# Loading part of the next sequence earlier in an attention and mixture-of-experts kernel, and moving two weight copies

## The chip, the cores and the metric

The kernel runs on one core of a Trainium2 chip. The metric is the device time of one execution in microseconds (us). The kernel before took 206.89 us (median of 3 executions, 206.02 to 209.92; with the fourth one that was taken beside the kernel after, 206.45). A core has five engines with their own instruction streams: TensorE for matrix multiplications, VectorE, ScalarE, GpSimd, and SyncE, which here only issues DMA. Data moves between HBM and on-chip memory (SBUF) over 16 DMA engines. These serve several queues. Two matter here. One is fed by SyncE (hardware queue, `q1`); it carries q, k, v and the outputs. The other is fed by GpSimd (software queue, `q0`); it carries the expert weights.

## The reference

Eight sequences of 576 tokens pass through attention with separate softmaxes on q and k, then through a mixture of experts (MoE) in which each whole sequence picks one of eight experts.

```python
q_s = softmax(q, over head_dim);  k_s = softmax(k, over the sequence)
kv  = einsum('bhsd,bhse->bhde', k_s, v)         # 64 x 64 per head
x   = einsum('bhsd,bhde->bhse', q_s, kv)        # -> (8, 576, 512)
pooled = x.mean(axis=1); e = argmax(pooled @ w_gate)   # one expert per sequence
out[b] = gate[b] * (relu(x[b] @ w1[e]) @ w2[e])  # w1 512x1024, w2 1024x512
```

## The kernel before

The kernel is one software pipeline. "Half n" means four heads of sequence n // 2, so halves 4 and 5 are sequence 2, and "load 4" brings q, k and v of half 4 (3 x 0.59 MB). While TensorE works on MoE of sequence b, the attention of sequence b + 1 is threaded between its matmuls. MoE b is cut into 17 pieces, and a table says which helper is emitted at which *tick*; ticks 17 b to 17 b + 17 belong to MoE b. Each engine's instructions stand in the program in the order in which the helpers emitted them, and an instruction that waits holds those behind it.

```python
    def load(n, names="qkv"):                    # SyncE: 3 DMAs into in_pool
        ...
    def cast_v(n, on_act=False):                 # GpSimd: v to 16 bit; waits for v's DMA
        ...
    def scale_q(n, eng):
        sum_q(n)                                 # VectorE: row sums, reciprocals (qsi)
        mul_q(n, eng)                            # GpSimd: eq * qsi, 2.12 us
    ...
    def load_w2(b):                              # GpSimd issues w2 of the expert of b, in two halves
        w2_src = moe_w2[ds(seqs[b]["e_val"], 1)].rearrange("o (c p) n -> p (o c) n", p=128)
        for hf in range(2):
            cs = slice(4 * hf, 4 * hf + 4)
            issued[b].append(
                nc.gpsimd.dma_start(out=w2_all[:, b % NS, cs], in_=w2_src[:, cs], **seqs[b]["kw"])
            )
        part_loads(b)
    ...
    def hold_loads(b):                           # SyncE reads a few bytes of w1 of b: SyncE waits until they are there
        nc.sync.dma_start(out=held, in_=w1_all[64:65, b, ND - 1, F - 8:F])
    ...
    def fetch(b, w_all, part):                   # VectorE: copies half of w1 or w2 from the slot where the expert lies
        ...
        copy = nc.vector.tensor_copy(
            out=w_all[:, b % NS, cs, fs],
            in_=w_all[:, ds(seqs[b]["src"], 1), cs, fs].rearrange("p o c f -> p (o c) f"),
        )
```

The weights stay in four slots. If the expert of sequence b lies in an older slot, no DMA is made and `fetch` copies it; if it was just loaded, the copy runs all the same, from the slot to itself. So TensorE always waits for the copy, and the copy waits for the DMA. The held read is the means of giving the weights the DMA engines first: SyncE, and all loads behind it, stand until w1 has landed.

The schedule that the change touches:

```python
    at_gate(0.2, 1)               # gate of sequence 1, and the issue of its w1 by GpSimd
    at(0.4, hold_loads, 1)
    at(0.4, load, 4)
    at(0.4, load, 5)
    at(0.4, load, 6)
    at(0.4, load, 7)
    ...
    at(13, load_w2, 1)
    ...
    places = [(20, 24.5), (29.7, 35), (41, 46), (56, 61), (73, 78), (90, 95)]
    for b in range(2, B):
        for i in range(2):
            n, t = 2 * b + i, places[b - 2][i]
            at(t, kvt_step, n)                    # TensorE: attention of half n
            ...
            at(t - 5.35, exp_q, n)
            at(t - (5.35 if n < 8 else 8), cast_v, n)
            at(t - 4.7, scale_q, n, nc.gpsimd)
        ...
        at_gate(places[b - 2][1] + (4.7 if b < 4 else 5), b)
    for b in range(1, B):
        for part in range(2):
            at(NU * b - 2.5 + 0.2 * part, fetch, b, w1_all, part)
            at((17.5, 38.3, NU * b + 4.5)[min(b, 3) - 1] + 0.2 * part, fetch, b, w2_all, part)
```

The softmax here doesn't subtract the row's maximum and nothing guards it: scores larger than these inputs give would overflow.

Of the kernel before, what the change touches and what calls it, by code (L numbers as in the profile page):

```python
# [19 lines left out]
def kernel(  # L20
# [15 lines left out]
    nc = tc.nc  # L36
# [3 lines left out]
    F = moe_w1.shape[2]  # L40
# [4 lines left out]
    ND = D // 128  # L45
# [17 lines left out]
    def bank(tag):  # L63
        return psum.tile([128, 1024 if tag == "x" else 512], FP32, name=tag, tag=tag, bufs=BUFS[tag])
# [17 lines left out]
    held = consts.tile([1, 8], FP16)  # L82
# [7 lines left out]
    w1_all = consts.tile([128, NS, ND, F], FP16, name="w1_all")  # L90
    w2_all = consts.tile([128, NS, NF, D], FP16, name="w2_all")
# [8 lines left out]
    def pair_src(t, b, i):  # L100

        return t[b].rearrange("(n i g) (p j) d -> i (g p) n (j d)", i=2, n=2, p=64)[i]
# [8 lines left out]
    def load(n, names="qkv"):  # L111
        if n >= 2 * B:
            return
        b, i = divmod(n, 2)
        for name in names:
            x = in_pool.tile([128, 2, J * Dh], FP32, name=f"{name}_in")
            nc.sync.dma_start(out=x, in_=pair_src({"q": q, "k": k, "v": v}[name], b, i))
            ins[n, name] = x.rearrange("p n (j d) -> p n j d", j=J)

    def exp_q(n):  # L120
        eq = e_pool.tile([128, J, 2, Dh], FP16, name="eq")
        nc.scalar.activation(out=eq.rearrange("p j n d -> p n j d"), in_=ins.pop((n, "q")), func=AF.Exp)  # L122
        halves[n] = {"eq": eq, "qt": {}, "kv": {}}

    def cast_v(n, on_act=False):
        dst = v_aug[n % NVB][:, :, 1:].rearrange("p j (n d) -> p n j d", n=2)
        if on_act:
            nc.scalar.copy(dst, ins.pop((n, "v")))
        else:
            nc.gpsimd.tensor_copy(out=dst, in_=ins.pop((n, "v")))  # L130

    def exp_k(n):
        ek = e_pool.tile([128, J, 2, Dh], FP16, name="ek")
        nc.scalar.activation(out=ek.rearrange("p j n d -> p n j d"), in_=ins.pop((n, "k")), func=AF.Exp)  # L134
        halves[n]["ek"] = ek

    def sum_q(n):
        qs = stat.tile([128, J, 2], FP32, name="qs")
        nc.vector.tensor_reduce(out=qs, in_=halves[n]["eq"], op=ALU.add, axis=AX.X)  # L139
        qsi = stat.tile([128, J, 2], FP32, name="qsi")  # L140
        nc.vector.reciprocal(out=qsi, in_=qs)  # L141
        halves[n]["qsi"] = qsi
        if n < 4:

            qhl = stat.tile([128, J, 2, 2], FP16, name="qhl")
            nc.vector.tensor_copy(out=qhl[:, :, 0], in_=qsi)
            nc.vector.tensor_tensor(out=qhl[:, :, 1], in0=qsi, in1=qhl[:, :, 0], op=ALU.subtract)
            halves[n]["qhl"] = qhl

    def mul_q(n, eng):  # L150
        eq, qsi = halves[n]["eq"], halves[n]["qsi"]
        eng.tensor_tensor(  # L152
            out=eq, in0=eq, in1=qsi.unsqueeze(3).to_broadcast([128, J, 2, Dh]), op=ALU.mult,
        )
# [57 lines left out]
    def kv_step(n):  # L212
        kv_mm(n)
        for g in range(2):
            kv_out(n, g)

    def t_step(n):
        t_mm(n)
        for g in range(2):
            t_out(n, g)  # L220
# [8 lines left out]
    def x_step(n, g):  # L229
        b, i = divmod(n, 2)  # L230
        c = 2 * i + g
        if c == 0:
            xt = xt_pool.tile([128, ND, S], FP16, name="xt")
            seqs.setdefault(b, {})["xt"] = xt
            if b > 1:
                seqs[b]["pooled"] = gat_pool.tile([128, ND], FP32, name="pooled")
        xt, pooled = seqs[b]["xt"], seqs[b].get("pooled")
        kvs, qts = halves[n]["kv"], halves[n]["qt"]
        px = bank("x")
        warm(FILL.get(("x", c, b), 0), px[:, 640:768])  # L240
        nc.tensor.matmul(px[:, 0:SM], lhsT=kvs[g], rhs=qts[g][:, 0:SM], start=True, stop=True)  # L241
        nc.tensor.matmul(px[:, SM:S], lhsT=kvs[g], rhs=qts[g][:, SM:S], start=True, stop=True)  # L242
        if b < 2:

            if c == 0 or n == 3:
                nc.vector.tensor_copy(out=xt[:, c, :], in_=px[:, 0:S])
            else:
                nc.scalar.copy(xt[:, c, :], px[:, 0:S])
        elif n < 8 and g:
            nc.scalar.activation(out=xt[:, c, :], in_=px[:, 0:S], func=AF.Copy, accum_out=pooled[:, c:c + 1])  # L250
        else:
            nc.vector.tensor_tensor_reduce(  # L252
                out=xt[:, c, :], in0=px[:, 0:S], in1=ones_f32.to_broadcast([128, S]),
                scale=1.0, scalar=0.0, op0=ALU.mult, op1=ALU.add, accum_out=pooled[:, c:c + 1],
            )

    def q_sum_step(n):


        b, i = divmod(n, 2)  # L260
        eq, qhl = halves[n]["eq"], halves[n]["qhl"]
        if i == 0:
            seqs.setdefault(b, {})["qb"] = [bank("mm"), bank("ht")]
            seqs[b]["qbar"] = gat_pool.tile([128, ND, 2, 4], FP16, name="qbar")
        qbar = seqs[b]["qbar"]
        warm(FILL["qsum", n], seqs[b]["qb"][1][:, 256:384])
        for g in range(2):
            c = 2 * i + g
            r = slice(64 * g, 64 * g + 64)
            qb = seqs[b]["qb"][g][:, 4 * i:4 * i + 4]  # L270
            for j in range(J):
                nc.tensor.matmul(
                    qb, lhsT=eq[r, j], rhs=qhl[r, j].rearrange("p h n -> p (h n)"), start=(j == 0), stop=(j == J - 1)
                )
            nc.vector.tensor_copy(out=qbar[:, c, 0], in_=qb)
            nc.vector.tensor_tensor(out=qbar[:, c, 1], in0=qb, in1=qbar[:, c, 0], op=ALU.subtract)
# [84 lines left out]
    def part_loads(b):  # L361
        for load_inst in issued[b]:
            for copy in copies.get(b - 1, ()):
                apart(load_inst, copy)

    def load_w2(b):
# [8 lines that stand above are left out]
    def warm(count, pw=None):  # L375

        if pw is None:
            pw = bank("ht")[:, 0:128]
        width = pw.shape[1]
        for n in range(count):  # L380
            nc.tensor.matmul(pw, lhsT=ident, rhs=blkmask[:, 0:width], start=True, stop=True)  # L381

    def hold_loads(b):

        nc.sync.dma_start(out=held, in_=w1_all[64:65, b, ND - 1, F - 8:F])

    def gate_exp(b):
        ex = gat_pool.tile([1, E], FP32, name="ex")
# [93 lines left out]
    NU = 17  # L482
    ticks = {}

    def at(t, fn, *args):
        ticks.setdefault(t, []).append((fn, args))
# [8 lines left out]
    at(2, t_step, 2)  # L495
    at_gate(0.2, 1)
    at(0.4, hold_loads, 1)
    at(0.4, load, 4)
    at(0.4, load, 5)
    at(0.4, load, 6)  # L500
    at(0.4, load, 7)
# [8 lines left out]
    at(0.3, gate_exp, 0)  # L510
    at(1.2, gate_value, 0)
    at(2.2, gate_spread, 0)
    places = [(20, 24.5), (29.7, 35), (41, 46), (56, 61), (73, 78), (90, 95)]
    for b in range(2, B):
        for i in range(2):
            n, t = 2 * b + i, places[b - 2][i]
# [11 lines left out]
    for b in range(1, B):  # L528
        for part in range(2):
            at(NU * b - 2.5 + 0.2 * part, fetch, b, w1_all, part)  # L530
            at((17.5, 38.3, NU * b + 4.5)[min(b, 3) - 1] + 0.2 * part, fetch, b, w2_all, part)
    times = sorted(ticks)
    done = [0]

# [13 lines left out]
    with tc.manual_schedule(engines={ET.PE, ET.DVE, ET.Activation, ET.Pool, ET.SP}):  # L548

        warm(80)  # L550
        exp_q(0)
        sum_q(0)
        q_sum_step(0)
        mul_q(0, nc.vector)
        exp_k(0)
        exp_q(1)
        cast_v(0)
        sum_q(1)
        load(3)
        t_step(0)  # L560
        q_sum_step(1)
        mul_q(1, nc.gpsimd)
        kv_step(0)
        exp_k(1)
        cast_v(1, True)
        x_step(0, 0)
        exp_q(2)
        kv_step(1)
        t_step(1)
        exp_k(2)  # L570
        pool_step(0)
        gate_step(0)
        x_step(0, 1)
        sum_q(2)
        exp_q(3)
        q_sum_step(2)
        x_step(1, 0)
        kv_mm(2)
        exp_k(3)
        x_step(1, 1)  # L580
        sum_q(3)
        for g in range(2):
            kv_out(2, g)
        cast_v(3)
        load_w2(0)
        q_sum_step(3)
        kv_step(3)
        for b in range(B):
            for m, _ in enumerate(moe(b)):
                run_ticks(NU * b + m + 1)  # L590
# [30 lines left out]
```

## Time and profile before

| | before |
|---|---|
| time, median | 206.89 us |
| span of the profiled execution | 204.1 us, granted clock 0.954 |
| TensorE busy | 178.6 us (88%) |
| MoE 0, 1, 2, 3 begin at | 27.45, 47.45, 77.36, 103.67 us |
| TensorE first uses w2 of sequence 1 at | 62.17 us |
| first half of w2 of sequence 1 landed, second half | 44.72, 47.31 us |

"MoE b begins" is the first w1 matmul of sequence b. Landings are the times at which the last of the 16 DMA engines raised the transfer's semaphore.

These rows of the profile's page cut the span into 40 slices of 5.1 us. A digit is the busy share in tenths, and PEclk is TensorE's granted clock in tenths:

```profile
PE   6798998995999839898869789999998899999990
PEclk9967899999699996999969999999999999999998
DMA  5999999999999799917999937966999967994055
```

TensorE is busy nearly everywhere, so a gain can only come from its few dips. The DMA engines are full without a break until about 66 us. The prediction shows the waits behind the dips.

### The profile page before, as it was taken

The page shows a single profiled execution, that of the slowest core. Times are in us where ns is not written, and L with a number is a line of the kernel's source. Part 1 is how long each engine was busy: PE and PEld are TensorE (multiplying, and loading weights), DVE is VectorE, ACT ScalarE, POOL GpSimd, SP SyncE. Part 2 cuts the span into 40 slices and gives each one's busy share as a digit, 9 for nine tenths or more (in the row PEclk, how much of TensorE's full clock was granted, in tenths as well). Part 3 has the DMA queues.
Part 4 walks back from the last instruction along what each step waited for, and adds up shares of the span by engine and source line. Part 5 has one row for each costly group of instructions (what it writes and reads, how often), then busy time and mean ns, then how long its engine had stood idle before and what let it go on. Part 6 is the DMA issues. An engine that isn't in the chain of part 4 may idle for free.

```text
span 204.1 us, 4940 instructions
## 1 busy us (share of the span) xinstructions
PE 178.6 (88%) x1882; PEld 101.8 (50%) x1882; DVE 115.6 (57%) x344; ACT 113.8 (56%) x182; POOL 64.3 (32%) x71
## 2 busy tenths in 40 slices
PE   6798998995999839898869789999998899999990
PEld 6776864443455424454335445555554455455440
DVE  0678877223667582997457666896689673121000
ACT  2668527744777644783437523982596146445540
POOL 2061915000763353347404260424175406000000
PEclk9967899999699996999969999999999999999998
DMA  5999999999999799917999937966999967994055
GB/s 180 378 389 391 165 167 194 184 213 392 394 386 358 163 347 405 390 39 110 230 295 296 365 98 189 328 189 226 267 315 202 206 137 126 197 207 168 0 112 122
DMA packets 29735, 48.58 MB, mean 238 GB/s; under 512 B 4112, under 2 KB 11280, under 8 KB 29712
## 3 DMA queue, kind: packets, MB, share of 16 engines
q1 hardware_dynamic: 19472, 37.76, 55.3%
q0 software_dynamic: 8544, 10.49, 31.7%
q10 hardware_dynamic: 1696, 0.02, 0.7%
q8 instruction: 15, 0.25, 0.5%
q14 instruction: 8, 0.07, 0.1%
HBM read 61.88 MB, written 9.44 MB: 349 GB/s over the span
## 4 chain that ended last, share of the span: by engine, by line
PE 41%; DMA 31%; DVE 16%; issue 4%; ACT 3%; POOL 0%; SPq 0%; ACTq 0%; POOLq 0%; DVEq 0%
PE mm L451 15%; PE mm L432 13%; DMA w_all<-in_moe_w_dram 13%; DMA q_in<-in_q_dram 9%; DMA v_in<-in_v_dram 5%; DVE qs L139 4%; DMA wg_sb<-in_moe_w_gate_dram 3%; DVE w_all L415 3%; PE mm L466 2%; DMA out_dram<-osb 2%; PE x L241 2%; PE kv L179 2%; DVE qt L209 2%; DVE kv L189 2%; PE ht L437 2%
## 5 line engine op out<-in xcount | busy, mean ns | idle before, releaser
L432 PE MATMUL mm<-xt,w_all 128*128 128x512 f16 x256 | 68.1, 397 | 4.8 <-DVE w_all L415 2.4
L451 PE MATMUL mm<-w_all,hsb 128*128 128x512 f16 x256 | 60.1, 379 | 0.0
L441 ACT ACTIVATE hsb<-mm 128x512 f16<-128x512 f32 x64 | 37.8, 595 | 21.7 <-PE mm L432 20.3
L458 ACT ACTIVATE osb<-mm,gate 128x512 f32<-128x512 f32 x32 | 22.0, 687 | 41.9 <-PE mm L451 37.3
L415 DVE COPY w_all<-w_all 128x2048 f16 x28 | 29.5, 1053 | 21.5 <-DMA w_all<-in_moe_w_dram 17.1
L451 PEld LDWEIGHTS <-hsb 128*128 128x128 f16 x256 | 22.9, 98 | 26.1
L152 POOL TENSOR_TENSOR eq<-eq,qsi 128x1152 f16<-128x1152 f16 x13 | 28.0, 2152 | 24.7 <-DVE qsi L141 22.1
L432 PEld LDWEIGHTS <-w_all 128*128 128x128 f16 x256 | 21.3, 101 | 24.6 <-issue 6.5
L130 POOL CAST va<-v_in 128x1152 f16<-128x1152 f32 x15 | 19.7, 1310 | 33.4 <-DMA v_in<-in_v_dram 33.3
L139 DVE TENSOR_REDUCE qs<-eq 128x18 f32<-128x1152 f16 x16 | 21.5, 1344 | 9.8 <-ACT eq L122 9.5
L437 PEld LDWEIGHTS <-w_all 128*128 128x128 f16 x256 | 16.8, 101 | 16.4 <-issue 2.2
L349 POOL DMA_DIRECT2D w_all<-in_moe_w_dram x18 | 8.3, 460 | 49.4 <-DMA w_all<-in_moe_w_dram 21.1
L122 ACT ACTIVATE eq<-q_in 128x1152 f16<-128x1152 f32 x16 | 18.5, 1159 | 6.9 <-DMA q_in<-in_q_dram 6.9
L241 PE MATMUL x<-qt,kv 128*128 128x512 f16 x32 | 12.6, 393 | 8.8 <-DVE pooled L252 6.5
L252 DVE CUSTOM_DVE_ANT_0 xt<-x,ones_f 128x576 f16<-128x576 f32 x20 | 14.8, 738 | 7.3 <-PE x L242 7.3
L134 ACT ACTIVATE ek<-k_in 128x1152 f16<-128x1152 f32 x16 | 18.6, 1162 | 0.5 <-DMA k_in<-in_k_dram 0.5
L437 PE MATMUL ht<-xt,w_all 128*128 128x64 f16 x256 | 18.4, 196 | 0.0
L381 PEld LDWEIGHTS <-ident 128*128 128x128 f16 x202 | 14.3, 116 | 2.5 <-POOL ident masks.py:199 1.6
L381 PE MATMUL ht<-blkmask,ident 128*128 128x128 f16 x170 | 13.5, 254 | 1.9 <-POOL blkmask L73 1.9
L179 PE MATMUL kv<-va,ek 64*128 64x129 f16 x288 | 11.9, 224 | 0.0
L189 DVE SCALAR_TENSOR_TENSOR kv<-kv,icv,blkmask 128x128 f16<-128x128 f32 x32 | 11.2, 351 | 1.2
L187 DVE RECIPROCAL icv<-kv 128x1 f32<-128x1 f32 x32 | 5.1, 159 | 10.9 <-PE kv L201 10.3
(77 smaller groups left out, 141.6 us busy)
## 6 DMA issues: line engine op xcount, KB each, us to landing
w_all<-in_moe_w_dram POOLq DMA_DIRECT2D x30, 512.0 KB
q_in<-in_q_dram SPq DMA_DIRECT2D x16, 576.0 KB, 6.1
k_in<-in_k_dram SPq DMA_DIRECT2D x16, 576.0 KB, 6.9
v_in<-in_v_dram SPq DMA_DIRECT2D x16, 576.0 KB, 8.4
out_dram<-osb SPq DMA_DIRECT2D x64, 128.0 KB, 5.6
w_all<-in_moe_w_dram POOLq DMA_DIRECT2D x4, 256.0 KB
out_dram<-osb_t SPq DMA_DIRECT2D x16, 64.0 KB, 2.8
gate<-gt ACTq DMA_DIRECT2D x8, 0.5 KB, 5.7
```

The source lines that it names most:

```text
L122: nc.scalar.activation(out=eq.rearrange("p j n d -> p n j d"), in_=ins.pop((n, "q")), func=AF.Exp)
L130: nc.gpsimd.tensor_copy(out=dst, in_=ins.pop((n, "v")))
L134: nc.scalar.activation(out=ek.rearrange("p j n d -> p n j d"), in_=ins.pop((n, "k")), func=AF.Exp)
L139: nc.vector.tensor_reduce(out=qs, in_=halves[n]["eq"], op=ALU.add, axis=AX.X)
L152: eng.tensor_tensor(out=eq, in0=eq, in1=qsi.unsqueeze(3).to_broadcast([128, J, 2, Dh]), op=ALU.mult,)
L381: nc.tensor.matmul(pw, lhsT=ident, rhs=blkmask[:, 0:width], start=True, stop=True)
L415: copy = nc.vector.tensor_copy(out=w_all[:, b % NS, cs, fs], in_=w_all[:, ds(seqs[b]["src"], 1), cs, fs].rearrange("p o c f -> p (o c) f"),)
L432: nc.tensor.matmul(phm, lhsT=w1_sb[:, c, fsl], rhs=xt[:, c, 0:SM], start=(c == 0), stop=(c == ND - 1),)
L437: nc.tensor.matmul(pht[:, fc * ST:(fc + 1) * ST], lhsT=w1_sb[:, c, fsl], rhs=xt[:, c, SM:S], start=(fc == 0 and c == 0), stop=(fc == NF - ...
L441: nc.scalar.activation(out=hsb[:, fc, 0:SM], in_=phm, func=AF.Relu)
L451: nc.tensor.matmul(po, lhsT=hsb[:, fc, st * 128:st * 128 + 128], rhs=w2_sb[:, fc, :], start=(fc == 0), stop=(fc == NF - 1),)
L458: nc.scalar.mul(osb, po, gate)
```

## The change

The intent was to remove the wait of 2.08 us near 50 us. Half 4 is to be loaded in the middle of the weights: a held read of the first half of w2 of sequence 0, then load 4, then the rest as before. Its attention moves from MoE 1 (ticks 20, 24.5) into the end of MoE 0 and early MoE 1 (17, 25). And the copies of w2 of sequences 1 and 2 move to ticks at which GpSimd is not scaling, since a VectorE copy and a GpSimd scaling stretch one another (in the kernel before, copies take up to 2.22 us beside a scaling and 0.69 alone, and a scaling 2.56 us beside copies and 2.12 alone).

```diff
     def hold_loads(b):
-        nc.sync.dma_start(out=held, in_=w1_all[64:65, b, ND - 1, F - 8:F])
+        src = w1_all[64:65, b, ND - 1, F - 8:F] if b else w2_all[64:65, 0, 0, 0:8]
+        nc.sync.dma_start(out=held, in_=src)
@@
     at(0.4, hold_loads, 1)
-    at(0.4, load, 4)
     at(0.4, load, 5)
@@
-    places = [(20, 24.5), (29.7, 35), (41, 46), (56, 61), (73, 78), (90, 95)]
+    places = [(17, 25), (30, 35), (42, 47), (57, 62), (73, 78), (90, 95)]
@@
-            at((17.5, 38.3, NU * b + 4.5)[min(b, 3) - 1] + 0.2 * part, fetch, b, w2_all, part)
+            at((23.7, 36.2, NU * b + 4.5)[min(b, 3) - 1] + 0.2 * part, fetch, b, w2_all, part)
@@
         load_w2(0)
+        hold_loads(0)
+        load(4)
```

Line `at(13, load_w2, 1)` is untouched. But the cast of v of half 4 is emitted 5.35 ticks before its attention and the scaling 4.7 ticks before. With the attention at tick 17 these fall on 11.65 and 12.3, ahead of 13. GpSimd's order changes without a line about it.

## The prediction

> **What bounds the kernel now.** I read the page first. Of a 204.1 us span TensorE is busy 178.6 us (88%), but the chain that ended last gives it only 41% and the DMA queues 31%. So TensorE is the floor, and what can be gained or lost are its idle stretches and what holds them. I then read the chain in order of time between 31 and 70 us (columns: start, length, what):
>
> ```profile
> 32.81 9.24 DMA w_all<-in_moe_w_dram
> 42.06 0.80 SPq L385
> ...
> 42.97 5.90 DMA q_in<-in_q_dram
> 48.89 1.16 ACT eq L122
> 50.05 0.39 ACT osb L458
> 50.45 12.47 DMA q_in<-in_q_dram
> 62.93 4.35 DMA out_dram<-osb
> 67.29 0.74 ACT xt L250 x2
> 68.08 0.36 PE x L296 x8
> ```
>
> From 22 to 66 us this is one stream of DMA: weights of sequences 0 and 1, the held read that waits for w1 of sequence 1 (42.06), four half-sequences of q, k, v, and the first outputs, whose buffers ScalarE needs again before it can evict x and gate 2 can run (68.08). The DMA windows show the stream without a hole: 192 GB/s in 36 to 44 us (the weight queue, counted after the cast to 16 bit, so about 385 of HBM reads), 393 GB/s in 47 to 63 us.
>
> Then TensorE in order of time, its long waits:
>
> ```profile
> 50.68 1.02 PE L432 MATMUL mm<-xt,w_all 128*128 128x512 f16 x4 [2.08 <-ACT osb L458]
> ...
> 76.91 0.58 PE L241 MATMUL x<-qt,kv 128*128 128x512 f16 x1 [3.65 <-DVE pooled L252]
> ...
> 103.67 1.89 PE L432 MATMUL mm<-xt,w_all 128*128 128x512 f16 x4 [2.44 <-DVE w_all L415]
> ```
>
> After each of the three the four matmuls take up to 1.9 us instead of 1.03 for some 3.4 us. The first is what the change goes for: ScalarE stands 3.37 us at exp of q of sequence 2, which landed at 48.89, and the eviction behind it holds TensorE. The second is the vector engine's copy of w1 of sequence 2, held by GpSimd's scaling:
>
> ```profile
> 73.52 2.12 POOL L152 TENSOR_TENSOR eq<-eq,qsi 128x1152 f16<-128x1152 f16 x1 [1.17 <-DVE qsi L141]
> ...
> 73.97 2.22 DVE L415 COPY w_all<-w_all 128x2048 f16 x1 [0.62 <-DVE qsi L141]
> ```
>
> The copy ends just after the scaling does; alone it takes 0.69 us. The third is w1 of sequence 3 landing at 102.8 us. After 120 us TensorE has about 1.3 us of gaps left, so what happens before 120 us is carried to the end.
>
> **What the Trainium skill says.** (1) "DMA: Bandwidth & Descriptors", section "Queues, rings and completion order": each DMA engine takes turns between the queues it has work for. The trace agrees; the DMA view of 102 to 112 us, in which weights and loads overlap:
>
> ```profile
> q1 hardware_dynamic: 967, 2.02, 58.7%
> q0 software_dynamic: 929, 0.93, 54.4%
> ```
>
> 0.93 MB of weights in 10 us (1.86 MB of HBM reads) beside 2.02 MB: equal shares, and a weight load takes twice its time alone. (2) "SBUF — State Buffer", section "SBUF: two separate sides": VectorE in a two-port mode and GpSimd exclude each other for a whole instruction. The 2.22 us copy above agrees. (3) "TensorE: Matmul & The Clock Gate", Part 1: after an idle window of some 3.4 us the clock is halved for a window. The trace has three such windows after 30 us, each of 3.4 us, behind the three waits above.
>
> **The change, part by part.** It adds one small held read; every other instruction stays, in another order. I read the order of the built program on each engine.
>
> (a) Load 4 (q, k, v of the first half of sequence 2, 3 x 0.59 = 1.77 MB) is issued when the first half of w2 of sequence 0 has landed, 33.1 us in the semaphore records, instead of 42.97. Data starts about 1.3 us after the issue at 34.0, so at 35.3. At that moment 0.88 MB of w1 of sequence 1 is left in the weight queue (1.75 MB of reads). Both share 0.387 MB/us, so both end near 44.6. The slowest engine lands 1.7 to 2.7 us after that (w1's 3.15 MB were through at 39.1 and landed at 42.05): w1 of sequence 1 and v at about 46.8, q at 41, k at 44. Exp of q then runs at 43.8 without a wait, and the 2.08 us hole with its slow window, some 4 us, goes.
>
> (b) The price is in GpSimd's order. Before, w2 of sequence 1 is issued at once after w1:
>
> ```profile
> 32.08 1.35 POOL L349 DMA_DIRECT2D w_all<-in_moe_w_dram  x2 [5.80 <-issue]
> 33.53 1.50 POOL L371 DMA_DIRECT2D w_all<-in_moe_w_dram  x2
> ```
>
> Now the cast of v of load 4 and its scaling stand ahead of it: v at 46.8, cast to 48, scaling (2.12 us) to about 50.5, so w2 of sequence 1 is issued at 50.6 instead of 33.5 and its data flows from 52. The loads 5, 6, 7 wait for w1 of sequence 1: held read at 46.8, data from 49.0. So between 44.6 and 49.0 the DMA engines have next to nothing to do: a hole of about 4.4 us in a stream that had none.
>
> (c) From 49.0 there are 5.31 MB of loads and 2.1 MB of reads for w2: 7.4 / 0.387 = 19.1 us, so the loads end at 68.1 instead of 62.7. The first outputs, behind them in the same queue, land at about 72.0 instead of 66.6: +5.4 us.
>
> (d) w2 of sequence 1 shares with the loads: 1.05 MB at 0.0945 MB/us is 11.1 us, so its halves are through at 57.7 and 63.3 and land at about 60 and 65.5. TensorE without a wait would be at its first use near 59 us. It stands about 3 us before the first half (the copy also meets the scaling of load 5) and 2 us before the second, and reaches the second half of the first output tile at 66.2. Before, this was 63.1 (62.17 plus four matmuls, 0.95): +3 us. The 2 us won in the first half of MoE 1 are gone by there.
>
> (e) Gate 2 waits for ScalarE's x, that for an eviction whose buffer is in flight until 72.0: 72.0 + 0.69 + 0.84 = 73.5 instead of 68.08, so +5.4. From gate 2 to MoE 2 is the same chain of VectorE as before (about 7.5 us from the attention step of load 6 to the next x), plus half an output tile placed ahead of it, 0.95, and a second copy ahead of x, 0.69, less some gate work now done earlier, 0.7. MoE 2 starts some 6 us late.
>
> (f) The part that should win: the copies of w2 of sequence 2 took 3.87 us for two at 85.44 beside a scaling and sat ahead of gate 3; they move two places up and should take 1.4. Gate 3 could come 1.9 us sooner, but GpSimd must first scale and cast load 8 and 9, which now come later; the issue of w1 of sequence 3 wins 0.6 to 0.9, and so does MoE 3. Attention of sequence 5, one place later, fills the 1.05 us wait at 115.5 with useful matmuls: another 1.0. Together about 1.7 us.
>
> Sum: +6 - 1.7 = +4.3 us. Sequence 3 and later are bound by TensorE alike in both, so it is carried to the end: 206.9 + 4.3 = 211.2. Estimates (a) to (e) rest on waits in series that may overlap better than I can count, which takes a little off: 210.8.
>
> **The rivals.** First, *the gain arrives whole*: q of sequence 2 is early, 4 us of hole and slow clock go, gate 3 comes 1.9 us sooner: 206.9 - 4 - 2 = about 201. The 3.37 us wait of ScalarE for q speaks for it. Against it: it only permutes a stream of DMA that is full, and gate 2 hangs on the end of that stream. Second, *it is hidden*: the hole is smaller than I think, because w1's engines finish one after another over 2 us (its records run from 40.1 to 42.05), and TensorE's early gain pays for the rest: about 206 to 208. Third, *the slow clock multiplies it*: the new holes (3, 2, 2.5 us) each bring their own slow window of 1.7 us, not hidden behind the next wait: 213 to 215.
>
> **Range and chances.** I put the middle at 210.8; eight in ten from 206.0 to 214.5. The line at 2% slower is 211.0, close to my middle, so slower and same are nearly even: 0.46 and 0.46. Faster by 2% needs 202.8, the first rival whole: 0.08.
>
> **What would show it.** In the profile after: the wait of 2.08 before the second block of MoE 1 is gone; GpSimd's issue of w2 of sequence 1 near 50 us; a hole in the DMA row of the page at some 44 to 49 us; TensorE waiting for VectorE's w2 copy at about 60 and 65 us; gate 2 near 73 us; MoE 3's first wait shorter than 2.44. I am wrong if w2 of sequence 1 lands before 60 us (then weights get more than half the engines, or GpSimd comes free sooner), if the DMA row shows no hole, or if gate 2 comes at 68 in spite of it.

## The result

| | before | after |
|---|---|---|
| time, median | 206.45 us (205.92 to 209.92, 4 executions) | 216.84 us (215.71 to 219.32, 4 executions) |
| ratio of the fast runs | 1 | 1.0494, 95% interval 1.0425 to 1.0563 |
| span of the profiled execution, clock | 204.1 us, 0.954 | 215.0 us, 0.956 |
| MoE 1 begins, lasts until MoE 2 | 47.45, 29.91 us | 48.27, 40.34 us |
| MoE 2 begins, lasts until MoE 3 | 77.36, 26.31 us | 88.61, 26.05 us |
| MoE 3 begins | 103.67 us | 114.66 us |
| first use of w2 of sequence 1 | 62.17 us | 68.71 us |
| gate 2 | 68.08 us | 77.42 us |

A ratio is the mean time of one kernel's fast runs over that of the other's in the same rounds, so it is not quite the quotient of the medians. Executions over 1.5% slower than the fastest of the same kernel are left out of the means. One of the four runs after (219.32) is left out, and so is the slowest of the four before (209.92): the means are 216.46 and 206.28.

The kernel became 5% slower. The difference of the two stages says where: 40.34 - 29.91 = 10.4 us lie in MoE 1, as much as the whole loss.

One caution for all that follows. MoE 0 begins at another time in each profile (26.76 us in the kernel after, 27.45 in the kernel before, up to 31.63 in the experiments), although TensorE's work up to there is the same. Where a microsecond or two matters, times of two profiles are therefore counted from the start of MoE 0. So counted, MoE 0 lasts 21.51 us after the change and 20.00 before: TensorE waits 1.43 us for the copy of w1 before MoE 1. The earlier start of MoE 0 (0.69) hides part of this in the table.

The chain's shares changed from PE 41, DMA 31, VectorE 16 to this line of the page:

```profile
PE 36%; DVE 24%; DMA 23%; ACT 7%; issue 5%; POOL 1%; SPq 1%; POOLq 0%; DVEq 0%; ACTq 0%
```

The page's rows for the kernel after (slices of 5.4 us):

```profile
PE   6786879979802983598996988998999899999990
PEclk9999999999985699579999999999999999999998
DMA  6999999969998089970599995996499985997045
```

In the PE row the hole is at the twelfth and thirteenth digit, 0 and 2: TensorE nearly empty from 59 to 70 us. Under it PEclk falls to 8, 5 and 6, the slow clock after the idle stretch (granted at half from 62.9 to 73.2 us). The dip that the change aimed at is gone, and the slow window of 52 us with it. The DMA row has only one weak digit near 43 to 48 us (6), but a 0 just after the hole, from 70 to 75 us.

This is the chain in order of time, whose columns are start, length, what:

```profile
51.03 16.85 DMA w_all<-in_moe_w_dram
...
67.96 0.71 DVE w_all L416
...
68.71 1.89 PE mm L452 x4
...
77.45 0.31 PE x L296 x8
...
83.36 2.52 DVE w_all L416
85.91 1.53 DVE w_all L416
```

Where the chain before ran through q loads and outputs to gate 2, it now runs through one transfer, w2 of sequence 1: 16.85 us, then the copy, TensorE and, without a further wait on outputs, gate 2 at 77.45.

GpSimd's timeline shows why that transfer began so late (in brackets the idle time before, and what ended it):

```profile
46.50 1.17 POOL L130 CAST va<-v_in 128x1152 f16<-128x1152 f32 x1 [13.75 <-DMA v_in<-in_v_dram]
47.62 2.56 POOL L152 TENSOR_TENSOR eq<-eq,qsi 128x1152 f16<-128x1152 f16 x1
50.13 1.66 POOL L371 DMA_DIRECT2D w_all<-in_moe_w_dram  x2
```

GpSimd stood 13.75 us for v of half 4, with the issue of w2 behind it in its order. Before, the same issue was made at 33.53.

And these are the lines of VectorE and TensorE that ended the hole:

```profile
67.96 1.42 DVE L416 COPY w_all<-w_all 128x2048 f16 x2 [11.97 <-DMA w_all<-in_moe_w_dram]
```

```profile
68.71 1.89 PE L452 MATMUL mm<-w_all,hsb 128*128 128x512 f16 x4 [10.55 <-DVE w_all L416]
...
88.16 0.58 PE L241 MATMUL x<-qt,kv 128*128 128x512 f16 x1 [5.46 <-DVE pooled L252]
```

TensorE waited 10.55 us in one piece. The two copies ran back to back, 1.42 us for both, at 67.96, although the first half had landed at 62.17 and only the second at 67.88. In the trace the first copy waits on the semaphores of both halves. The second line is the wait before MoE 2, which grew from 3.65 to 5.46 us.

### The profile page after: what moved, and what is told of

Same layout as the page of the kernel before. It is cut to its first block, busy times and chain, and to the rows that moved or that the text cites. A ratio compares the mean times of both kernels' runs of the same rounds, so it can differ in the third digit from the quotient of the medians.

```text
span 215.0 us, 4941 instructions
## 1 busy us (share of the span) xinstructions
PE 176.6 (82%) x1882; PEld 99.6 (46%) x1882; DVE 117.0 (54%) x344; ACT 113.7 (53%) x182; POOL 64.0 (30%) x71
## 4 chain that ended last, share of the span: by engine, by line
PE 36%; DVE 24%; DMA 23%; ACT 7%; issue 5%; POOL 1%; SPq 1%; POOLq 0%; DVEq 0%; ACTq 0%
DMA w_all<-in_moe_w_dram 15%; PE mm L452 14%; PE mm L433 10%; DVE w_all L416 6%; DVE qs L139 5%; DMA v_in<-in_v_dram 5%; DMA q_in<-in_q_dram 4%; PE kv L179 3%; DVE kv L189 3%; DVE qt L209 2%; PE x L241 2%; ACT hsb L442 2%; PE mm L467 2%; ACT eq L122 2%; ACT ek L134 1%
## 5 line engine op out<-in xcount | busy, mean ns | idle before, releaser
L452 PE MATMUL mm<-w_all,hsb 128*128 128x512 f16 x256 | 61.6, 386 | 10.6 <-DVE w_all L416 10.6
L433 PE MATMUL mm<-xt,w_all 128*128 128x512 f16 x256 | 65.8, 388 | 3.1 <-DVE w_all L416 3.1
L433 PEld LDWEIGHTS <-w_all 128*128 128x128 f16 x256 | 20.8, 99 | 21.7 <-DVE w_all L416 3.6
L130 POOL CAST va<-v_in 128x1152 f16<-128x1152 f32 x15 | 18.9, 1262 | 24.7 <-DMA v_in<-in_v_dram 24.6
L438 PEld LDWEIGHTS <-w_all 128*128 128x128 f16 x256 | 16.5, 99 | 15.7 <-issue 1.1
L349 POOL DMA_DIRECT2D w_all<-in_moe_w_dram x18 | 8.3, 460 | 46.8 <-DMA w_all<-in_moe_w_dram 17.8
L252 DVE CUSTOM_DVE_ANT_0 xt<-x,ones_f 128x576 f16<-128x576 f32 x20 | 14.8, 740 | 6.4 <-PE x L242 6.4
L381 PEld LDWEIGHTS <-ident 128*128 128x128 f16 x202 | 12.2, 105 | 2.2 <-POOL ident masks.py:199 1.6
L381 PE MATMUL ht<-blkmask,ident 128*128 128x128 f16 x170 | 11.6, 234 | 1.9 <-POOL blkmask L73 1.9
L179 PE MATMUL kv<-va,ek 64*128 64x129 f16 x288 | 12.4, 230 | 0.0
```

The source lines that it names most:

```text
L130: nc.gpsimd.tensor_copy(out=dst, in_=ins.pop((n, "v")))
L381: nc.tensor.matmul(pw, lhsT=ident, rhs=blkmask[:, 0:width], start=True, stop=True)
L433: nc.tensor.matmul(phm, lhsT=w1_sb[:, c, fsl], rhs=xt[:, c, 0:SM], start=(c == 0), stop=(c == ND - 1),)
L438: nc.tensor.matmul(pht[:, fc * ST:(fc + 1) * ST], lhsT=w1_sb[:, c, fsl], rhs=xt[:, c, SM:S], start=(fc == 0 and c == 0), stop=(fc == NF - ...
L452: nc.tensor.matmul(po, lhsT=hsb[:, fc, st * 128:st * 128 + 128], rhs=w2_sb[:, fc, :], start=(fc == 0), stop=(fc == NF - 1),)
```

## The experiments

Nine kernels ran, one of them twice. The first theory, called G in the expectations, is GpSimd's order: the late issue of w2 of sequence 1 is the loss, and the rest of the change is harmless or good. Its rivals are that the early load itself disturbs the DMA stream, or that the moved copies do the harm. "Before" had these medians on the same chips: 206.44 us (four kernels), 207.29 (four), 205.80 (two).

### 1. w2 issued first

```diff
-    at(13, load_w2, 1)
+    at(11.6, load_w2, 1)
```

The kernel after, with GpSimd's old order for this one issue.

> The changed kernel with one tick moved: the load of w2 of sequence 1 stands on GpSimd ahead of the cast and scaling of load 4, as in the kernel before; load 4 stays early. Theory G (GpSimd's order holds back w2 of sequence 1, from 32.9 to 50.1 us, and with it TensorE for 10.55 us): w2 issued near 33 us, landed by 52, no wait of TensorE at its first use near 59, time 204 to 208 us. Rival L (the early load 4 itself is at fault, since it only permutes a full DMA stream and delays w1): TensorE waits for w1 or the casts instead, and the time stays at 212 or more.

Measured: 207.75 us (207.56 to 209.00), ratio 1.0107 (1.0036 to 1.0178). GpSimd issues w2 before it waits for v:

```profile
35.60 1.49 POOL L371 DMA_DIRECT2D w_all<-in_moe_w_dram  x2
50.60 1.21 POOL L130 CAST va<-v_in 128x1152 f16<-128x1152 f32 x1 [13.50 <-DMA v_in<-in_v_dram]
```

The hole is gone and MoE 1 lasts 29.90 us, against 40.34 in the kernel after and 29.91 before. What remains in TensorE's timeline is small waits that the early attention brings, and a longer one before MoE 2:

```profile
51.86 0.70 PE L179 MATMUL kv<-va,ek 64*128 64x129 f16 x18 [0.59 <-POOL va L130]
53.94 0.44 PE L201 MATMUL kv<-ident,eq 64*128 64x64 f16 x18 [1.37 <-POOL eq L152]
...
79.56 0.59 PE L241 MATMUL x<-qt,kv 128*128 128x512 f16 x1 [4.62 <-DVE gt L396]
```

So the order of one issue accounts for 1.0494 - 1.0107 = 0.0387, or some 8 of the 10 us of the ratio. The gain that was hoped for is not there either: even so mended, the change is about 1% slower than the kernel before. This 1% is also all that is left for the rivals on balance: the early load, the moved places and the moved copies are all still in this kernel (a gain of one could hide a loss of another).

### 2. The early load alone

```diff
 (kernel before)
-    at(0.4, load, 4)
+    hold_loads(0)      # held read of w2 of sequence 0, as in the change
+    load(4)            # instead of behind the held read of w1 of sequence 1
```

> The kernel before with nothing but the early load 4 and its held read; places and copies as before, so that GpSimd's order is unchanged. Theory G: the wait of 2.08 us before the second block of MoE 1 goes and nothing takes its place, 202 to 206 us. Rival L: slower than before by 4 us or more, 210 or over.

Measured: 207.52 us (206.53 to 209.47), ratio 1.0107 (1.0025 to 1.0190). This missed: theory G had 202 to 206 us, a gain of up to 4, and nothing was won; the 4 us of loss of the rival did not come either. Load 4 was issued 7.5 us sooner (35.50 against 42.97), but v of half 4 was cast at 50.25 instead of 52.03. Load 4 and the weights then shared the DMA engines, and w2 of sequence 1 landed at 49.87 and 55.79 instead of 44.72 and 47.31. The first copy of w2 waited for both halves, and VectorE with it:

```profile
55.87 1.42 DVE L416 COPY w_all<-w_all 128x2048 f16 x2 [3.64 <-DMA w_all<-in_moe_w_dram]
```

TensorE then stood 2.05 us for the scaling and 2.60 us for VectorE's next work, which replaces the 2.08 us that went:

```profile
54.58 0.44 PE L201 MATMUL kv<-ident,eq 64*128 64x64 f16 x18 [2.05 <-POOL eq L152]
59.68 0.47 PE L241 MATMUL x<-qt,kv 128*128 128x512 f16 x1 [2.60 <-DVE qt L209]
```

The DMA stream was full. Bringing one transfer forward pushed another back, and the same copy stood at its end.

### 3. The new order with the load at its old place

```diff
 (kernel after)
+    at(0.4, load, 4)        # behind the held read of w1 of sequence 1 again
-        hold_loads(0)
-        load(4)
```

> The changed kernel with load 4 put back behind the held read of sequence 1; places and copies stay as changed. Theory G: v of load 4 lands later, so w2 of sequence 1 is issued later still (near 54 us) and the time is worse than the changed kernel's, 218 to 224 us. Rival L: back to 205 to 209 us.

Measured: 220.12 us (218.88 to 222.80; one slow run), ratio 1.0644 (1.0557 to 1.0730). As expected: v of half 4 comes later, so w2 of sequence 1 is issued at 54.81 and lands at 71.50. A later issue costs more, and the early load is what kept the change from being worse than it was.

### 4. Without the copy of w2 of sequence 1

```diff
 (kernel after)
+            if b > 1:
                 at((23.7, 36.2, NU * b + 4.5)[min(b, 3) - 1] + 0.2 * part, fetch, b, w2_all, part)
```

With this draw of inputs the result stayed right, since the copy of sequence 1 only goes from the slot to itself. TensorE now waits for each half's own DMA, not for a copy that waits for both.

> The changed kernel without the copy of w2 for sequence 1 alone (on these data its expert is loaded fresh, so the copy is one of a slot onto itself and the result stays right). The program's first copy waits for both halves of the load, not for its own; without it TensorE waits for each half by itself. If that shared wait costs what the step (d) of the prediction left out: first use at 62.2 instead of 68.7, second half at 67.9 instead of 72.1, MoE 2 and the end 4 us sooner, 212 to 214 us. If only the second half counts because the attention step between hides the first: under 1.5 us gained, 215 or more.

Measured: 214.83 us (213.38 to 217.20; one slow), ratio 1.0407 (1.0319 to 1.0495); the profiled run was slow, so its times in us are only roughly those of a fast run. The one wait became two:

```profile
64.69 1.48 PE L452 MATMUL mm<-w_all,hsb 128*128 128x512 f16 x4 [3.98 <-DMA w_all<-in_moe_w_dram]
...
70.18 3.57 PE L452 MATMUL mm<-w_all,hsb 128*128 128x512 f16 x8 [2.45 <-DMA w_all<-in_moe_w_dram]
```

The ratios differ by 1.0494 - 1.0407 = 0.0087, about 1.8 us, between the two ranges expected; the intervals of the two overlap. So the joint wait of the copy may be a real term, but a small one, and these runs do not separate it from none. Landing late is the large one.

### 5. The copies of w2 of sequence 2 alone

```diff
 (kernel before)
-            at((17.5, 38.3, NU * b + 4.5)[min(b, 3) - 1] + 0.2 * part, fetch, b, w2_all, part)
+            at((17.5, 36.2, NU * b + 4.5)[min(b, 3) - 1] + 0.2 * part, fetch, b, w2_all, part)
```

> The kernel before with nothing but the copies of w2 of sequence 2 moved two places up (38.3 to 36.2), clear of the scaling that made two of them take 3.87 us. Step (f) of the prediction: gate 3 itself comes about 1.9 us sooner, but the issue of w1 of sequence 3 on GpSimd wins only 0.6 to 0.9, since a scaling and a cast stand ahead of it; the two copies take 1.4 us; time 0.3 to 1 us better, 205.3 to 206.3. If the slow copies did hold MoE 3: 2 us or more better, 204.4 or less. If they only fill idle time of VectorE: 206.4 unchanged.

Measured: 209.10 us (208.16 to 212.13; one slow), ratio 1.0063 (0.9990 to 1.0136), so no gain that could be seen. The copies do take less (0.68 and 0.65 us), but they stand ahead of VectorE's work for the next attention. TensorE then waits where it had waited 0.79 us (at 85.58):

```profile
89.11 0.43 PE L241 MATMUL x<-qt,kv 128*128 128x512 f16 x1 [2.01 <-DVE pooled L252]
...
118.51 0.38 PE L241 MATMUL x<-qt,kv 128*128 128x512 f16 x1 [3.38 <-DVE qt L209]
```

The second line was a wait of 1.05 us before. The wait of 2.44 us at MoE 3 did vanish, as hoped, and these took it back. That the second comes from the moved copies is not shown: it grew in experiment 9 too, to 2.31 us, where they were not moved.

### 6. w2 issued between cast and scaling

```diff
 (kernel after)
-    at(13, load_w2, 1)
+    at(12, load_w2, 1)
```

> The changed kernel with the load of w2 of sequence 1 one place up on GpSimd, behind the cast of load 4 but ahead of its scaling. A dose of theory G: issue 2.5 us sooner (47.6 instead of 50.1 us from the span's start), but no more than that, so first use of w2 near 66 instead of 68.7 and the time 214 to 215.5 us, between the changed kernel's 216.8 and the 207.8 of the run in which it is issued first. If the time is set elsewhere (both halves, or the loads' backlog), it stays at 216 or more.

Measured: 215.29 us (211.60 to 218.97), but only one of four executions counted as fast (211.60). In its profile, which is slow, w2 was issued at 48.75, landed at 61.30 and 67.04, and TensorE waited 7.02 us. The issue came 1.25 us after v had landed, against 3.78 in the kernel after: the 2.5 us that were expected. Counted from the start of MoE 0 it came 3.8 us sooner and the second half landed 3.2 us sooner, since v too was there 1.2 us earlier. What that is worth in time these runs cannot say. That the scaling is the smaller part of the delay is read from the fast profile of the kernel after: GpSimd stood 13.75 us for v, and the scaling behind it took 2.56.

### 7 and 8. Loads 6 and 7 behind w2, and the same again

```diff
 (kernel after)
+    def hold_w2(b):
+        nc.sync.dma_start(out=held, in_=w2_all[64:65, b, NF - 1, D - 8:D])
@@
-    at(0.4, load, 6)
-    at(0.4, load, 7)
@@
     at(13, load_w2, 1)
+    at(13.1, hold_w2, 1)
+    at(13.2, load, 6)
+    at(13.2, load, 7)
```

This gives w2 of sequence 1 the DMA engines nearly to itself.

> The changed kernel with loads 6 and 7 held back until w2 of sequence 1 has landed (one more held read), GpSimd's order as changed. It tells the late issue from the sharing with the loads: if the sharing doubles w2's transfer, it now takes 8 to 10 us from issue to landing instead of 17.7, it is landed at 59 to 60, TensorE's wait of 10.55 falls to under 3 us, and the time is 209 to 213 (loads 6 and 7 now come late for ScalarE, which takes some back). If the late issue alone counts, transfer and wait stay and the time is 217 or more.

Measured: 213.02 us (208.69 to 213.16), of which again only one was fast (208.69). The same kernel a second time:

> The kernel of the run with loads 6 and 7 behind w2 once more, since only one of its executions fell in the fast state (208.7), and that one decides how much of the wait is owed to loads 6 and 7 taking turns with w2 in the DMA queues. If the sharing is a main term, the fast executions are at 208.5 to 211, some 6 to 8 us below the kernel after. If they cluster at 213, it is worth 3 to 4 us and the issue behind the scaling is the larger term.

Measured: 210.02 us (209.47 to 211.94), ratio 1.0177 (1.0079 to 1.0276), with the kernel after at 1.0494. The profile: w2 of sequence 1 was issued at 51.35, landed at 59.84 and 62.37, so 11.0 us after the issue instead of the 17.75 of the kernel after (8 to 10 were expected in experiment 7). The wait at its first use, expected under 3 us:

```profile
63.20 1.04 PE L456 MATMUL mm<-w_all,hsb 128*128 128x512 f16 x4 [3.81 <-DVE w_all L420]
```

Counted from the start of MoE 0, the issue is as late as in the kernel after (22.57 and 23.37 us), and the intervals of the two ratios do not overlap. So about two thirds of the loss, 1.0494 - 1.0177 = 0.0317 or some 6.5 us, need both causes at once: an issue that comes late, and then loads of later sequences that stand in the same DMA engines. Two of the six times (211.66, 211.94) lie above the 208.5 to 211 that were expected for a main term, the other four within.

### 9. The scaling behind the copy

The experiments keep pointing at VectorE's copy of w1 of sequence 2, which runs beside a GpSimd scaling just before MoE 2. The next kernel leaves the change aside and reorders only these in the kernel before: the scaling of half 7 comes after both copies.

```diff
 (kernel before)
-            at(t - 4.7, scale_q, n, nc.gpsimd)
+            at(31.75 if n == 7 else t - 4.7, scale_q, n, nc.gpsimd)
@@
-            at(NU * b - 2.5 + 0.2 * part, fetch, b, w1_all, part)
+            at(NU * b - 2.5 + 0.1 * part, fetch, b, w1_all, part)
```

> The kernel before with the row sum and the scaling of load 7 set behind the copies of w1 of sequence 2 and the eviction of x, so that the copies run free of GpSimd (1.4 us for two instead of 2.22 and 0.68) and x of load 6 is evicted 2 to 2.5 us sooner. It asks whether a collision of this kind, moved by order alone, is worth what the idea of the change hoped for: TensorE's wait of 3.65 us before MoE 2 falls to 1 to 1.5 us and the slow window behind it goes; the scaling now comes late for the attention step of load 7 and takes 1 to 1.5 us back; time 202.5 to 205.5. If that comes back whole, 206 to 207.

Measured: 204.52 us (203.30 to 205.51, six executions), ratio 0.9871 (0.9822 to 0.9920). It beats both kernels, by less than the 2% that would be called faster. The 3.65 us before MoE 2 are gone. In their place TensorE waits briefly for the scaling, which is now later:

```profile
79.76 0.44 PE L201 MATMUL kv<-ident,eq 64*128 64x64 f16 x18 [0.46 <-POOL eq L152]
```

Two other waits are longer than in the kernel before: 1.94 us instead of 0.57 at gate 2, and 2.31 instead of 1.05 in MoE 3 (at 114.34).

### 10. Both repairs on the kernel after

The kernel after with `at(11.6, load_w2, 1)` of experiment 1 and the two lines of experiment 9.

> The kernel after with w2 of sequence 1 issued ahead of the cast and scaling of load 4 (as in the first experiment, 1.0107 of before) and the scaling of load 7 behind the copies of w1 of sequence 2 (which alone took the kernel before to 0.987). In the first experiment a wait of 4.62 us stood before MoE 2, for that copy. If the two repairs add, that wait goes and the time is 203.5 to 205.5, as good as the scaling repair alone. If the other waits of the early load (0.5, 0.6 and 1.4 us in MoE 1) stay as the price of the change: 205 to 207. If the 4.62 us were held by something else than the scaling: 206.5 to 209.

Measured: 205.81 us (203.94 to 207.05; one slow), ratio 0.9932 (0.9786 to 1.0078): unclear against the kernel before. The profiled run was the slow one; in it the wait before MoE 2 was 2.33 us, not 4.62. The early load is not ruled out as neutral, but it adds nothing to the repair of experiment 9 that these runs could see.

### What orders the kernels

One row per kernel, in order of when the second half of w2 of sequence 1 landed, counted from the start of MoE 0. All of these profiles are fast:

| kernel | w2 landed, both halves (us) | second half, from the start of MoE 0 (us) | TensorE's wait for it (us) | MoE 1 lasts (us) | ratio |
|---|---|---|---|---|---|
| before | 44.72, 47.31 | 19.9 | none | 29.91 | 1 |
| w2 issued first (1) | 51.00, 56.61 | 27.1 | none | 29.90 | 1.0107 |
| the early load alone (2) | 49.87, 55.79 | 28.0 | none | 31.39 | 1.0107 |
| loads 6 and 7 behind w2 (8) | 59.84, 62.37 | 33.6 | 3.81 | 34.40 | 1.0177 |
| after | 62.17, 67.88 | 41.1 | 10.55 | 40.34 | 1.0494 |
| load 4 at its old place (3) | 65.99, 71.50 | 42.5 | 7.36, and 3.84 before MoE 1 | 39.14 | 1.0644 |

TensorE in the kernel after had no more w1 work from 58.2 us on, which is 31.4 after the start of MoE 0. Landings up to 28.0 cost no wait at w2. Past that, each later landing costs, and the order of the landings is the order of the times. An order of six kernels proves no cause by itself; experiments 1 and 8, which move the landing by one edit each, carry that.

## Why the prediction was right and wrong

The prediction gave 210.8 us with a range to 214.5. Measured were 216.84. It gave slower and same equal chances. The path was right as far as the copy of w2: GpSimd's order, late w2, TensorE waiting for the copy. The step that failed is (d), TensorE's wait for w2 of sequence 1: 3 and 2 us counted, 10.55 measured. Step (e) had the wrong wait in front of gate 2 and too short a one behind it, and step (f) was taken for a gain that did not come.

**Step (a): half right.** The 2.08 us hole and its slow window went (though a wait of 1.43 us before MoE 1, which the prediction did not have, came in), and v of half 4 landed at 46.35, where 46.8 was predicted. That this number fits is luck, for two errors cancelled. Load 4 did not share the engines with w1 of sequence 1 from 35.3 on. Its data began 4.0 us after the issue, not 1.3: q was issued at 34.61, and the packets of its first 20 KB had started by 38.65. For 35 to 38 us the DMA view of the kernel after has:

```profile
q1 hardware_dynamic: 3, 0.00, 0.1%
```

The columns are packets, MB, and share of the 16 engines. The hardware queue moved nothing in these 3 us. When its data did flow, w1 of sequence 1 was nearly through, so that it hardly had to share; by 41.24 us 15 of the 16 engines had finished it. SyncE's held read started at 43.65, since the last engine finished only at 43.63. (One reading of this step is off: the weight queue's first 3.15 MB were through at 40.3 us in the kernel before, not at 39.1. Nothing else hangs on it.)

**Step (b): the order right, the start of the data wrong.** Issue predicted at 50.6, measured 50.13. The data was to flow "from 52". These are the DMA views of the kernel after, first for 50 to 54 us, then for 54 to 62 us:

```profile
q1 hardware_dynamic: 719, 1.56, 103.3%
```

```profile
q1 hardware_dynamic: 766, 1.66, 60.6%
q0 software_dynamic: 649, 0.65, 49.0%
```

In the first stretch there is no packet of the weight queue at all; the packets of its first 20 KB had started by 54.85. The equal shares of the second stretch were as predicted. The predicted hole in the DMA row, 44.6 to 49.0 us, was there but smaller: the traffic fell below 100 KB per us only from 44 to 46. What had to be carried afterwards was thus not more than predicted.

**Step (c): too large.** The loads and the outputs behind them were to come 5.4 us later than before. The last load landed at 67.70 instead of 65.89 and the second output at 68.47 instead of 66.60, 1.8 and 1.9 later, since the data of loads 5 to 7 flowed from 46 us on and not from 49.0. Sized so, with the waits of step (d) as they stood, the prediction would have come out lower and further off; that it lay no further from the result is luck.

**Step (d): the term that failed.** The halves were to land at 60 and 65.5. With data starting some 2.8 us later than assumed, 62.8 and 68.3 would follow; measured were 62.17 and 67.88. So the late start of the queue explains the whole miss of the landings. The waits were to be 3 and 2 us. They were 10.55 in one piece, 5.5 more. Part of that is the late landing. Part is that the first copy waits for both halves, which the prediction did not have; experiment 4, where each half is waited for alone, puts this at about 1.8 us, with intervals that overlap. The second half of the first output tile was reached at 72.10 instead of the predicted 66.2, or 5.9 late. The slow clock then took its share: the granted clock was at half from 62.9 to 73.2 us, and the first four w2 matmuls took 1.89 us where eight took 1.90 before.

**Step (e): another wait than predicted.** Gate 2 was to come at 73.5, held by output buffers. It came at 77.42, and the chain reaches it from the w2 copy, with no output in between. The output buffers no longer mattered because what stands in front of the gate was later than they: the last output of MoE 0 had landed at 70.91, and ScalarE's next eviction began only at 73.69. To the stretch from gate 2 to MoE 2 the prediction added 0.95 + 0.69 - 0.7 = 0.94 us; it grew by 1.9, from 9.28 to 11.19, nearly all of it in TensorE's wait before MoE 2 (3.65 to 5.46). There stands the known pair of the w1 copy and the scaling:

```profile
83.36 4.07 DVE L416 COPY w_all<-w_all 128x2048 f16 x2 [0.33 <-DVE qsi L141]
```

Two copies in 4.07 us, where one takes 0.69 alone. In the kernel before, x of half 6 (L252) stood between the two, and only the first held TensorE:

```profile
73.97 2.22 DVE L415 COPY w_all<-w_all 128x2048 f16 x1 [0.62 <-DVE qsi L141]
76.11 0.74 DVE L252 CUSTOM_DVE_ANT_0 xt<-x,ones_f 128x576 f16<-128x576 f32 x1
...
76.78 0.68 DVE L415 COPY w_all<-w_all 128x2048 f16 x1
```

Place 30 instead of 29.7 for half 6 puts x at tick 32, behind both copies (31.5 and 31.7). The prediction had this second copy, at 0.69 us, but it took 1.53, beside GpSimd's cast of the next v:

```profile
85.27 1.62 POOL L130 CAST va<-v_in 128x1152 f16<-128x1152 f32 x1
```

The copies ahead of x took 4.07 - 2.22 = 1.85 us more, and the wait grew by 1.81. Experiment 1 has both copies ahead of x too (3.20 us, the wait 4.62), which is the largest wait that its timeline shows. No experiment moved this place alone.

MoE 2 began 88.61 - 77.36 = 11.25 us late, where the prediction had 6. That experiment 9 removed this wait in the kernel before, and gained 1.3% by it, shows that the pair of copy and scaling is the cause there.

**Step (f): won on the way, not at the end.** MoE 3's first wait did shrink, from 2.44 to 1.64 us, and the MoE 2 stage is 0.26 us shorter. But the spans differ by 215.0 - 204.1 = 10.9, against 11.25 at MoE 2: 0.35 us came back where 1.7 were counted. The wait of 1.05 us that was to be filled was still 0.64 (at 126.61). For the copies experiment 5 suggests the reason: moved alone, the copies of w2 of sequence 2 win the wait at MoE 3 and lose it in two others, of which only the first is traced to them.

**The rivals.** "The gain arrives whole" is refuted, and by experiment 2 even for the early load alone. "The slow clock multiplies it", 213 to 215, was the nearest in number. It held in that a slow window followed the hole; that it was the main term is not shown. The clock did not lengthen the wait, it only slowed the work behind it.

**In sum.** The spans differ by 10.9 us where the sum had 4.3. Of the 6.6 us that were missing, 3.9 were there at gate 2 (77.42 against 73.5), from step (d); 1.3 came between gate 2 and MoE 2, from the end of step (e), which had also rounded its 6.3 to 6; and 1.35 did not come back in step (f). Of the loss itself, some 10 us by the ratio, some 8 hang on the one issue that slid behind a cast and a scaling (experiment 1). Some 6.5 of these are there because the loads of later sequences then use the DMA engines at the same time (experiment 8). Why a queue that joins a busy one needs some 4 us to move its first data is measured but not explained.

## What to carry to other kernels

When helpers move in a schedule, list for each engine what now stands behind what: an instruction that waits for a DMA holds everything behind it, and the dearest thing to hold is the issue of another DMA. A transfer moved forward in a full stream moves another one back, so ask which consumer of the displaced one has the least slack. And look up in the built program which semaphores a copy waits for: here one copy waited for two halves, and started when the second had landed.

## What the Trainium skill lacked or had wrong

- "DMA: Bandwidth & Descriptors", section "Queues, rings and completion order", says that an engine takes turns between the queues it has work for. Once both flow the traces agree (49.0% of the engines' time beside 60.6% in 54 to 62 us). It does not say that a queue joining late is not served at once. Counted from the issue to the start of the packets of its first 20 KB, with the other queue busy, load 4 needed 4.0 us in the kernel after and 3.8 to 4.4 us in experiments 1, 2, 6 and 8; w2 of sequence 1 needed 4.3 to 4.8 us in the kernel after and experiments 3, 6 and 7, and 2.9 in experiment 8. With the other queue empty (experiment 3) or nearly so (experiment 7) load 4 needed 1.2 and 1.3 us.
- The same page, section "Latency and other measured facts", says that two of the 16 engines are usually slower than the others, but gives no size for how long a wait then lasts. Here w1 of sequence 1 was through on 15 engines at 41.24 us and on the last at 43.63, and a held read waits for the last. Which engine that was the trace does not tell.
- "TensorE: Matmul & The Clock Gate", Part 1, which the prediction cites for an idle window of some 3.4 us, does not say how idle such a window has to be. In the kernel before the clock was halved at 52.32 us, and in the 3.4 us up to there TensorE had been busy for 1.36; its wait in them was 2.08 us.
